# First pair of an attention kernel: the order of its maxima, score blocks, P·V groups and loads

## The chip, the cores and the metric

The kernel runs on one core of a Trainium2 chip. The metric is device time in microseconds (us) from start to end of one launch. PE is TensorE (matmul), DVE is VectorE, ACT is ScalarE, POOL is GpSimd, and SP is the engine whose queue issues most DMAs here. Each engine works through its own instructions in the order in which they stand.

## The reference, cut to what matters

Attention with queries averaged in pairs, then two mixture-of-experts layers, of which this change touches nothing:

```python
q_pool = q.reshape(B, H, S // 2, 2, D).mean(axis=3)       # B 4, H 8, S 1152, D 64
scores = scale * np.matmul(q_pool, k.transpose(0, 1, 3, 2))
scores = scores - np.max(scores, axis=-1, keepdims=True)
attn = np.exp(scores)
attn = attn / (np.sum(attn, axis=-1, keepdims=True) + 1e-09)
x = np.matmul(attn, v)                                    # then moe(x), then soft moe
```

## The kernel before

The 32 heads go in 16 pairs (`p` 0 to 15, the two heads `j` of a pair side by side). All operands of a pair are split into a high part and a remainder: `KS` holds the keys' high part in its upper 64 rows and their remainder in the lower 64, `QS` the queries' high part twice, `QL` the queries' remainder, `KH` the keys' high part again. Three sets of these exist, and pair `p` uses set `p % 3`.

**Maxima.** A query's maximum has to be known before its exponentials. `maxpiece` makes one product of 128 queries with 384 keys on PE (line 198) and reduces it on DVE (line 200). A pair has 27 pieces: per head nine for queries 0 to 383 (blocks 0 to 2, pieces 0 to 17 of the two heads), three for block 3, and three for block 4, which the two heads share (through the tile `QB`). `maxred` gathers the results in `MXZ` (lines 207 and 209), a small matmul turns it round (`nps`, line 229 for the first pair, 216 for the others), and DVE writes the maxima as extra rows of `QL` (lines 236 and 241, or 218 and 221). Only then can the second matmul of a score block run.

**Score blocks.** A pair has 36 score blocks, one for each half of the queries (`u`), each of nine key blocks (`c`) and each head (`j`). Block number is called position below. A block is a matmul `S1` (line 247), a matmul `S2` (line 253, which needs `QL` with the maxima) and an exponential on ACT (line 257) into `e`. Three PSUM buffers hold blocks, three others hold pieces.

**P·V groups.** After every six blocks PE makes a group of twelve products with V (line 267), and POOL adds up the sums of `e` (lines 278 and 280, 1.4 us each).

**The order.** Everything stands as the loops write it: a table gives, for each position, what is issued behind that block. While the blocks of pair `p` run, the pieces of pair `p + 1` are worked off between them (in the first pair from position `P1[0]` on), the operands of pair `p + 2` are prepared (`prep`, whose functions are: two casts of K into `KC`, the addition of the queries, the cast `QC`, two remainders `KL`, the remainder `QLc`), and the inputs of pair `p + 3` are loaded. `KC`, `KL`, `QC` and `QLc` go to their places in `KS`, `KH`, `QS` and `QL` by DMAs from SBUF to SBUF (line 149), which SP issues one after the other.

**The start.** `first` loads and prepares pair 0 with no DMA copies, and prepares pair 1 (`prep1`). Before the loop the 18 pieces of blocks 0 to 2 of both heads are made and reduced, with a small filler matmul (`warm`) behind all but the first three. The four DMAs of lines 530, 531, 1479 and 1480 load small tables (`wgbd`, `modt`, `mb`); those of line 519 copy five rows of ones into the two other sets of `KH`.

Of the kernel before, what the change touches and what calls it, by code (L numbers as in the profile page):

```python
# [12 lines left out]
AX = mybir.AxisListType  # L13
# [25 lines left out]
QSTEP = 2  # L39
GS = 3  # L40
LAG = 3
EB = 9
CST = 3
P0 = (0, 6)
P1 = (11, 22)
SWARM = (0, 1, 1)
FE = (14, 16, 17)
PREP = (2, 8, 2, 8, 14, 20, 26)
PREP0 = (14, 16, 14, 18, 20, 24, 28)
MA1 = (0, 1, 2, 3, 4, 5, 6, 7, 9, 10, 11, 12, 13, 15, 16, 17, 18, 19, 21, 22, 23, 24, 25, 27)  # L50
MA = (0, 1, 3, 4, 5, 6, 7, 9, 10, 12, 13, 15, 16, 17, 18, 19, 21, 22, 23, 25, 27)
MB = (29, 30, 31, 33, 34, 35)
MR = (29, 32)
FA = (26, 28, 33)
FB = (14, 16, 17)
FC = 7
# [25 lines left out]
def attention(ctx, tc, g):  # L82
# [116 lines left out]
            slot = 4 * j + blk  # L199
        V.reduce_max(s["mxp"][:, slot, t:t + 1], mps[:, :384], axis=AX.X)  # L200

    def maxred(p, blks):
        s = st[p]
        Z = MXZ
        if min(blks) < 4:
            b0, b1 = min(blks), min(max(blks), 3) + 1
            V.reduce_max(Z[:, :, 64 + b0:64 + b1], s["mxp"][:, 0:8].rearrange("p (j b) t -> p j b t", j=2)[:, :, b0:b1], axis=AX.X)
        if 4 in blks:
            V.reduce_max(Z[:, :, 68:69], s["mxp"][:, 8:9].unsqueeze(1).to_broadcast([128, 2, 1, 3]), axis=AX.X)

# [9 lines left out]
        for j in range(2):  # L220
            V.tensor_mul(ql[64:69, j, 512:576], nv[:, j, 64 * j:64 * j + 64], mask[64:69, 4, 0:64])

    def maxrow0(p, spans):

        s = st[p]
        ql = s["QL"]
        nps = ps.tile([128, 512], F32, name="nps", tag="mx", bufs=3)
        for j in range(2):
            nc.tensor.matmul(nps[:69, j * 128:(j + 1) * 128], MXZ[:, j, :], ident, start=True, stop=True)
        for j in range(2):  # L230
            nv = nps[64:69, j * 128:(j + 1) * 128]
            for lo, hi in spans:
                blk, o = divmod(lo, 128)
                if (hi - lo) % 128 == 0:
                    a = (hi - lo) // 128
# [192 lines left out]
    def first():  # L428
# [66 lines left out]
        for m in range(3, 9):  # L495
            maxpiece(0, m)
            warm(SWARM[1])
        klo(P, 1, 0)
        qadd(P, 1, qq[0])
        qadd(P, 1, qq[1])  # L500
        klo(P, 1, 1)
        klo(P, 1, 2)
        for j in range(2):
            nc.scalar.copy(KH[0][0:64, j], kx[j][0:64])
        prep1 = prep(1, P)
        for j in range(2):
            ql(P, j, q2[0])
        load(2)
        for f in prep1[:4]:
            f()  # L510
        for j in range(2):
            qadd(P, j, q2[1])
            nc.scalar.copy(QB0[:, j, j * 64:(j + 1) * 64], qs0[:, j, 512:576])
            ql(P, j, q2[1])
        return prep1, warm

    prep1, warm = first()
    for i in (1, 2):
        nc.sync.dma_start(out=KH[i][64:69].bitcast(F32), in_=KH[0][64:69].bitcast(F32))
    prep1[6]()  # L520
    nc.gpsimd.memset(wgbd, 0.0)
    nc.gpsimd.memset(ones, 1.0)
    for m in range(9, NP0):
        maxpiece(0, m)
        warm(SWARM[2])
    maxred(0, [0, 1, 2])
    maxrow0(0, [(0, 256), (256, 288)])
    for f in prep1[4:6]:
        f()
    nc.sync.dma_start(out=wgbd[0:64, :, 0:E], in_=wg[0])  # L530
    nc.sync.dma_start(out=wgbd[64:128, :, E:2 * E], in_=wg[1])
    consts = g["route_consts"]()
# [1 line left out]
    for p in range(n + 1):  # L534
# [5 lines left out]
        mp = lambda q, m: (lambda: maxpiece(q, m))  # L540
        NP = len(pieces)
        if p == 0:
            for i, m in enumerate(range(NP0, NP)):
                at(P0[0] + i * P0[1] // 8, mp(0, m))
            at(P0[0] + P0[1] + 1, lambda: maxred(0, [3, 4]))
            at(P0[0] + P0[1] + 2, lambda: maxrow0(0, [(288, 384), (384, 512), (512, 576)]))
            for i, m in enumerate([24, 25, 26] + list(range(24))):
                at(P1[0] + i * P1[1] // NP, mp(1, m))
            for i in range(3):
                at(33 + i, mp(2, 24 + i))  # L550
        elif p + 1 < n:
            for pos, m in zip(MA1, range(24)) if p == 1 else zip(MA, range(3, 24)):
                at(pos, mp(p + 1, m))
            if p + 2 < n:
                for pos, m in zip(MB, (24, 25, 26, 0, 1, 2)):
                    at(pos, mp(p + 2, m))
# [2 lines left out]
                at(pos, f)  # L559
        if p < n:  # L560
            if p + 1 < n:
                late = 3 if p == 0 else 0
                at(MR[0] + late, lambda: maxred(p + 1, [0, 1, 2, 3, 4]))
                at(MR[1] + late, lambda: maxrow(p + 1))
            late = 4 if p in (0, n - 1) else 0
            at(FA[0] + late, lambda: fin0(p, 0))
            at(FA[1] + late, lambda: fin1(p, 0))
# [70 lines left out]
            break  # L638

        units = [(u, c, j) for u in range(2) for c in range(NKB) for j in range(2)]  # L640
        for z in units[:3]:
            S1(p, *z)
        for pos, z in enumerate(units):
# [12 lines left out]
                        queue.pop(0)[1]()  # L656
            if pos == LAG - 1 and p > 0:
                group(p - 1, 2 * NKB // GS - 1)
            elif pos >= 2 * GS and pos % (2 * GS) == LAG - 1:
                group(p, pos // (2 * GS) - 1)  # L660
            if pos == 3 and p + 3 < n:
                if p == 0:
                    load_v(2)
                load(p + 3)
# [962 lines left out]
```

## Time and profile before

| | |
|---|---|
| time, median of 3 runs | 829.63 us (827.89 to 830.55) |
| the profiled execution, own time | 833.58 us |
| its span | 831.9 us |
| PE busy over the span | 798.0 us (96%) |
| DVE busy | 571.0 us (69%) |
| ACT busy | 466.9 us (56%) |
| POOL busy | 542.3 us (65%) |

A row of a timeline gives the start in us, the duration in us, the engine, the line, the operation, out<-in with the tiles' names, and how many instructions were merged; in brackets stands the idle time of the engine ahead of it and what ended it. PE's rows overlap, since matmuls are pipelined: the distance between two starts tells more than the durations. A row of the windows gives a stretch and the busy time of each engine in it, and after them the granted clock of PE as a share of 2.4 GHz.

### The profile page before, as it was taken

Reading aid. Unit: us, or ns where it says so; the run is one execution under the profiler, and the core shown is the slowest. Engines: PE = TensorE matmul, PEld = TensorE weight load, DVE = VectorE, ACT = ScalarE, POOL = GpSimd, SP = SyncE. Lnnn points to the kernel's source line nnn. Section 1 sums busy time; section 2 is a strip of 40 time slices with the busy share of each in tenths; the row PEclk is TensorE's granted clock in tenths of the full one; section 3 lists DMA queues with packets and bytes.
Section 4 is the critical chain, followed back from the end, with each engine's and each line's share of the span. In section 5 each row is a group of like instructions: output and inputs, shape, how many; then the busy total and the mean of one; then the engine's idle time right before and its main releaser. Section 6 shows DMA issues by size and latency. Waiting matters only on the chain. (4 is left out here: it accounts for less than half of the span.)

```text
span 831.9 us, 16156 instructions
## 1 busy us (share of the span) xinstructions
PE 798.0 (96%) x5808; PEld 612.5 (74%) x5808; DVE 571.0 (69%) x1177; ACT 466.9 (56%) x1107; POOL 542.3 (65%) x501
## 2 busy tenths in 40 slices
PE   5799999999999999999999999999999999999997
PEld 4567777777677676777666668798898988887456
DVE  7587777668777976877878786665665666665252
ACT  5456565657756558666547872554654545553123
POOL 6778899999888977879879962445446454450100
PEclk9899999999999999999999999999999999999998
DMA  9776558684664585566453212677776877757897
GB/s 317 218 198 160 159 150 218 156 224 137 144 161 145 133 213 157 159 145 172 117 130 102 87 42 79 241 253 274 255 266 218 303 238 271 269 189 243 280 391 228
DMA packets 57898, 163.13 MB, mean 196 GB/s; under 512 B 14474, under 2 KB 21962, under 8 KB 53706
## 3 DMA queue, kind: packets, MB, share of 16 engines
q1 hardware_dynamic: 41460, 97.01, 41.3%
q0 software_dynamic: 13760, 47.60, 17.1%
q10 hardware_dynamic: 2592, 17.43, 5.8%
q8 instruction: 47, 0.77, 0.4%
q14 instruction: 39, 0.32, 0.1%
HBM read 110.71 MB, written 10.90 MB: 146 GB/s over the span
## 5 line engine op out<-in xcount | busy, mean ns | idle before, releaser
L280 POOL TENSOR_TENSOR acc<-acc,e 128x576 f32<-128x576 f32 x214 | 315.9, 1476 | 28.2 <-ACT e L257 13.7
L257 ACT ACTIVATE e<-sc 128x288 f32<-128x288 f32 x576 | 224.3, 411 | 142.3 <-PE sc L253 120.3
L200 DVE TENSOR_REDUCE mxp<-mps 128x1 f32<-128x384 f32 x432 | 220.2, 549 | 99.5 <-PE mps L198 94.3
L247 PE MATMUL sc<-QS,KS 128*128 128x288 f32 x576 | 185.0, 329 | 3.0 <-ACT e L257 2.8
L253 PE MATMUL sc<-QL,KH 69*128 69x288 f32 x576 | 169.8, 297 | 1.5 <-DVE QL L218 1.2
L267 PE MATMUL pv<-e,V 128*64 128x288 f32 x1152 | 162.4, 417 | 0.0
L247 PEld LDWEIGHTS sc<-QS,KS 128*128 128x128 f32 x576 | 109.0, 190 | 52.3 <-issue 26.7
L198 PE MATMUL mps<-KS,QS 128*128 128x384 f32 x384 | 134.7, 355 | 13.1 <-ACT QS L463 7.3
L727 POOL DMA_INDIRECT wraw<-in_w,widx x72 | 73.0, 1013 | 109.9 <-DVE wlo L749 92.5
L267 PEld LDWEIGHTS pv<-e,V 128*64 128x64 f32 x1152 | 74.6, 137 | 63.8 <-issue 25.9
L749 DVE TENSOR_TENSOR wlo<-wraw,whi 128x512 fp32r<-128x512 f32 x144 | 95.9, 689 | 22.6 <-ACT whi L748 19.8
L253 PEld LDWEIGHTS sc<-QL,KH 69*128 69x128 f32 x576 | 109.1, 190 | 1.9 <-DVE QL L218 1.4
L748 ACT CAST whi<-wraw 128x512 fp32r<-128x512 f32 x144 | 84.1, 619 | 14.8 <-DMA wraw<-in_w,widx 10.4
L198 PEld LDWEIGHTS mps<-KS,QS 128*128 128x128 f32 x384 | 73.9, 193 | 17.1 <-ACT QS L463 7.7
L757 PE MATMUL hp<-xh,whi 128*128 128x256 f32 x288 | 81.9, 284 | 0.4 <-ACT xh L743 0.4
L758 PE MATMUL hp<-xl,whi 128*128 128x256 f32 x288 | 80.9, 281 | 1.4 <-DVE xl L744 1.4
L759 PE MATMUL hp<-xh,wlo 128*128 128x256 f32 x288 | 80.6, 280 | 0.0
L764 ACT ACTIVATE hh<-hp 128x256 fp32r<-128x256 f32 x72 | 27.7, 385 | 80.5 <-PE hp L759 54.5
L278 POOL TENSOR_TENSOR acc<-e 128x576 f32<-128x576 f32 x31 | 45.0, 1450 | 35.9 <-ACT e L257 35.8
L765 DVE SCALAR_TENSOR_TENSOR hl<-hp,hh 128x256 fp32r<-128x256 f32 x72 | 30.5, 423 | 48.5 <-ACT hh L764 41.2
L771 PE MATMUL yp<-whi,hh 128*128 128x512 f32 x144 | 59.6, 414 | 0.2 <-ACT hh L764 0.2
L758 PEld LDWEIGHTS hp<-xl,whi 128*128 128x128 f32 x288 | 54.1, 188 | 4.8 <-DVE xl L744 2.2
(366 smaller groups left out, 1237.5 us busy)
## 6 DMA issues: line engine op xcount, KB each, us to landing
mw<-in_m2w ACTq DMA_DIRECT2D x16, 1024.0 KB
mw<-in_m2w SPq DMA_DIRECT2D x16, 1024.0 KB
V<-in_vT SPq DMA_DIRECT2D x16, 576.0 KB
KX<-in_kT SPq DMA_DIRECT2D x15, 576.0 KB
QX<-in_qT SPq DMA_DIRECT2D x15, 576.0 KB
KS<-KC SPq DMA_DIRECT2D x30, 288.0 KB
KH<-KC SPq DMA_DIRECT2D x30, 288.0 KB
QS<-QC SPq DMA_DIRECT2D x60, 144.0 KB
```

Source lines behind the costliest of these rows:

```text
L198: nc.tensor.matmul(mps[:, :384], s["QS"][:, j, blk * 128:(blk + 1) * 128], s["KS"][:, j, ks], start=True, stop=True)
L200: V.reduce_max(s["mxp"][:, slot, t:t + 1], mps[:, :384], axis=AX.X)
L247: nc.tensor.matmul(sc[:, :NU], s["KS"][:, j, c * 128:(c + 1) * 128], s["QS"][:, j, u * NU:(u + 1) * NU], start=True, stop=False)
L253: nc.tensor.matmul(sc[:, :NU], s["KH"][0:69, j, c * 128:(c + 1) * 128], s["QL"][0:69, j, u * NU:(u + 1) * NU], start=False, stop=True)
L257: nc.scalar.activation(s["e", u, c][:, j], sc[:, :NU], AF.Exp, scale=SM)
L267: nc.tensor.matmul(pv[j * 64:(j + 1) * 64, :NU], s["v"][:, j, c, :], e[:, j], start=(c == 0), stop=(c == NKB - 1))
L280: eng.tensor_add(s["acc", u], s["acc", u], s["e", u, c])
L748: nc.scalar.copy(hi, x)
L749: nc.vector.tensor_sub(lo, x, hi.bitcast(F32))
L757: nc.tensor.matmul(hp, wh[:, c], xh[:, k], start=(k == 0), stop=False)
L758: nc.tensor.matmul(hp, wh[:, c], xl[:, k], start=False, stop=False)
L759: nc.tensor.matmul(hp, wl[:, c], xh[:, k], start=False, stop=(k == DM // 128 - 1))
```

## The change

It touches the first pair alone, and the operands of the second pair that are prepared beside it.

- Ahead of the loop one piece less than half is made: pieces 0 to 9 instead of 0 to 17 (`NJ1 = 1`), and the maxima of head 0 alone are gathered and turned (`js`). The eight other pieces of head 1 stand behind positions 0 to 7, and its gathering behind position 7.
- The blocks of the first half come in another order: nine of head 0, then nine of head 1, where they alternated.
- Pieces 18 to 26 stand behind positions 9 to 15 (they stood behind 0 to 5), the second pair's 27 pieces behind positions 17 to 32 (they stood behind 11 to 32). The groups stand behind positions 14, 17, 20, 26 and 32 (8, 14, 20, 26 and 32).
- In `first` POOL makes `QL` of head 0 before the queries' additions of head 1. Of `prep1`, the remainders `KL` of the second pair move ahead of `QC`; `QC` stands behind position 4, `QLc` behind 5. So their copies stand behind the small tables in SP's queue.
- The preparation of the third pair starts later (`PREP0`); gathering and turning the second pair's maxima stand behind positions 32 and 33 (32 and 35); the loads of the fourth pair stand behind position 8 (3).

```diff
+PV0 = (14, 17, 20, 26, 32)
-P0 = (0, 6)
-P1 = (11, 22)
+P0 = (9, 6)
+P1 = (17, 16)
+NJ1 = 1
-PREP0 = (14, 16, 14, 18, 20, 24, 28)
+PREP0 = (19, 20, 16, 22, 24, 26, 30)
+MR0 = (32, 33)
...
         klo(P, 1, 0)
+        ql(P, 0, q2[0])
         qadd(P, 1, qq[0])
...
-        for j in range(2):
-            ql(P, j, q2[0])
-        load(2)
-        for f in prep1[:4]:
-            f()
-        for j in range(2):
-            qadd(P, j, q2[1])
+        ql(P, 1, q2[0])
+        load(2)
+        c = q2[1]
+        for j in range(2):
+            P.tensor_add(qs0[:, j, c], qx[:, j, 0, c], qx[:, j, 1, c])
+        for i in (0, 1, 2, 4, 5):
+            prep1[i]()
+
+        def rest(j):
+            nc.scalar.copy(QS[0][:, j, c], qs0[:, j, c])
             nc.scalar.copy(QB0[:, j, j * 64:(j + 1) * 64], qs0[:, j, 512:576])
-            ql(P, j, q2[1])
-        return prep1, warm
+
+        return [(1, lambda: rest(0)), (2, lambda: rest(1)), (3, lambda: ql(P, 0, c)), (3, lambda: ql(P, 1, c)), (4, prep1[3]), (5, prep1[6])], warm
...
-    for m in range(9, NP0):
+
+    maxred(0, [0, 1, 2], slice(0, 1))
+    for m in range(9, 9 + NJ1):
         maxpiece(0, m)
         warm(SWARM[2])
-    maxred(0, [0, 1, 2])
-    maxrow0(0, [(0, 256), (256, 288)])
+    maxrow0(0, [(0, 256), (256, 288)], (0,))
...
+            for pos, f in early:
+                at(pos, f)
+            for i, m in enumerate(range(9 + NJ1, NP0)):
+                at(i, mp(0, m))
+            at(7, lambda: maxred(0, [0, 1, 2], slice(1, 2)), lambda: maxrow0(0, [(0, 256), (256, 288)], (1,)))
...
+        if p == 0:
+            units[:18] = [(0, c, j) for j in range(2) for c in range(NKB)]
...
-            if pos == 3 and p + 3 < n:
+            if pos == (3 if p else 8) and p + 3 < n:
```

PE at the end of the start, before (`mps` is a piece, `nps` the turned maxima, `sc` a block by `S1` or, from `QL`, by `S2`; names end in buffer numbers, and `KS_138`, `KH_141`, `QS_144`, `QL_147` are the first pair's):

```order
L198 MATMUL mps<-KS_138,QS_144 128x384
L479 MATMUL warm<-ident 128x128
L229 MATMUL nps<-ident,MXZ 69x128 x2
L247 MATMUL sc<-QS_144,KS_138 128x288 x3
L253 MATMUL sc<-QL_147,KH_141 128x288
L198 MATMUL mps<-KS_138,QS_144 128x384 x2
L253 MATMUL sc<-QL_147,KH_141 128x288
```

PE at the same place after the change:

```order
L201 MATMUL mps<-KS_138,QS_144 128x384
L482 MATMUL warm<-ident 128x128
L232 MATMUL nps<-ident,MXZ 69x128
L250 MATMUL sc<-QS_144,KS_138 128x288 x3
L256 MATMUL sc<-QL_147,KH_141 128x288
L201 MATMUL mps<-KS_138,QS_144 128x384
L256 MATMUL sc<-QL_147,KH_141 128x288
```

The rows are alike but for one turned head instead of two; before, 18 pieces stand ahead of them, now 10, and the next pieces are head 1's.

SP's queue from the second pair's first copy to the first of the later loads, before (`KS_139`, `KH_142`, `QS_145` and `QL_148` are the second pair's):

```order
L149 DMA KH_142<-KC 64x1152
L149 DMA QS_145<-QC 64x576 x4
L149 DMA QB<-QC 64x64 x2
L519 DMA KH_142<-KH_141 5x2304
L519 DMA KH_143<-KH_141 5x2304
L149 DMA QL_148<-QLc 64x576 x2
L149 DMA KS_139<-KL 64x1152 x2
L530 DMA wgbd<-in_wg 64x4x8
L531 DMA wgbd<-in_wg 64x4x8
L1479 DMA modt<-in_mod 96x48
L1480 DMA mb<-in_mbias 96x16
L133 DMA V_162<-in_vT 128x1152
```

The same stretch of SP's queue after the change:

```order
L152 DMA KH_142<-KC 64x1152
L152 DMA KS_139<-KL 64x1152 x2
L526 DMA KH_142<-KH_141 5x2304
L526 DMA KH_143<-KH_141 5x2304
L535 DMA wgbd<-in_wg 64x4x8
L536 DMA wgbd<-in_wg 64x4x8
L1493 DMA modt<-in_mod 96x48
L1494 DMA mb<-in_mbias 96x16
L152 DMA QS_145<-QC 64x576 x4
L152 DMA QB<-QC 64x64 x2
L152 DMA QL_148<-QLc 64x576 x2
```

The `KL` copies went ahead, and the copies of `QC` into `QS` and `QB`, which were first, now stand behind the small tables.

PE where the second pair's pieces begin, before (`mps<-KC,QB` are the second pair's three shared pieces, which come first):

```order
L229 MATMUL nps<-ident,MXZ 69x128 x2
L267 MATMUL pv<-e,V_160 64x288 x6
L247 MATMUL sc<-QS_144,KS_138 128x288
L253 MATMUL sc<-QL_147,KH_141 128x288
L247 MATMUL sc<-QS_144,KS_138 128x288
L253 MATMUL sc<-QL_147,KH_141 128x288
L247 MATMUL sc<-QS_144,KS_138 128x288
L253 MATMUL sc<-QL_147,KH_141 128x288
L195 MATMUL mps<-KC,QB 128x384 x2
L247 MATMUL sc<-QS_144,KS_138 128x288
```

PE where they begin after the change:

```order
L232 MATMUL nps<-ident,MXZ 69x128 x2
L250 MATMUL sc<-QS_144,KS_138 128x288
L256 MATMUL sc<-QL_147,KH_141 128x288
L198 MATMUL mps<-KC,QB 128x384 x2
L270 MATMUL pv<-e,V_160 64x288 x6
L250 MATMUL sc<-QS_144,KS_138 128x288
L256 MATMUL sc<-QL_147,KH_141 128x288
```

Before, they stand behind position 11 and one group; now behind position 17, with one group ahead of them and the second right behind the first two.

## Rows read from the trace of the kernel before

**Rows 1.** Windows: stretch, busy us (instructions) of each engine, PE's clock, DMA, GB/s.

```profile
30.00:40.00 10.00, 6.78 (x28) 4.61 (x29) 2.30 (x6) 2.00 (x5) 5.24 (x5) 0.66 0.86 286
60.00:70.00 10.00, 10.00 (x72) 7.13 (x69) 7.35 (x13) 6.75 (x16) 8.36 (x10) 1.00 0.61 152
33.00:38.80 5.80, 5.58 (x20) 3.41 (x21) 1.12 (x2) 1.19 (x3) 1.52 (x2) 0.50 0.90 323
```

**Rows 2.** Timeline of PE over the first pair.

```profile
19.77 0.37 PE L253 MATMUL sc<-QL,KH 69*128 69x288 f32 x1 [0.31 <-ACT QB L513]
...
29.15 0.29 PE L253 MATMUL sc<-QL,KH 69*128 69x288 f32 x1
33.22 0.66 PE L198 MATMUL mps<-KS,QS 128*128 128x384 f32 x1 [3.78 <-DMA KS<-KL]
...
34.61 3.15 PE L267 MATMUL pv<-e,V 128*64 128x288 f32 x12
...
41.74 1.68 PE L267 MATMUL pv<-e,V 128*64 128x288 f32 x12
...
55.51 0.38 PE L216 MATMUL nps<-ident,MXZ 128*69 128x128 f32 x2
...
57.62 0.40 PE L253 MATMUL sc<-QL,KH 69*128 69x288 f32 x1 [1.21 <-DVE QL L218]
```

**Rows 3.** Timeline of DVE over the same stretch.

```profile
11.02 7.06 DVE L200 TENSOR_REDUCE mxp<-mps 128x1 f32<-128x384 f32 x15
18.18 0.17 DVE L207 TENSOR_REDUCE MXZ<-mxp 128x6 f32<-128x18 f32 x1
...
42.73 0.76 DVE L173 TENSOR_TENSOR KL<-KX,KC 128x576 fp32r<-128x576 f32 x1
...
46.42 1.52 DVE L173 TENSOR_TENSOR KL<-KX,KC 128x576 fp32r<-128x576 f32 x1
...
52.97 0.18 DVE L207 TENSOR_REDUCE MXZ<-mxp 128x8 f32<-128x24 f32 x1
```

**Rows 4.** Timeline of POOL.

```profile
13.70 1.98 POOL L466 TENSOR_TENSOR QL<-qs,QS 64x384 fp32r<-64x384 f32 x2
...
18.09 0.58 POOL L466 TENSOR_TENSOR QL<-qs,QS 64x192 fp32r<-64x192 f32 x1 [0.48 <-ACT QS L463]
...
19.69 0.59 POOL L466 TENSOR_TENSOR QL<-qs,QS 64x192 fp32r<-64x192 f32 x1 [0.46 <-ACT QS L463]
20.25 1.41 POOL L179 TENSOR_TENSOR QLc<-qs,QC 128x576 fp32r<-128x576 f32 x1
...
21.77 2.81 POOL L173 TENSOR_TENSOR KL<-KX,KC 128x576 fp32r<-128x576 f32 x2
...
44.40 1.43 POOL L278 TENSOR_TENSOR acc<-e 128x576 f32<-128x576 f32 x1 [2.18 <-ACT e L257]
```

**Rows 5.** Timeline of ACT.

```profile
14.03 1.24 ACT L153 CAST KC<-KX 128x576 fp32r<-128x576 f32 x2
```

**Rows 6.** Timeline of SP's queue: the DMAs as they are issued.

```profile
15.29 0.55 SPq L149 DMA_DIRECT2D KS<-KC  x1
...
19.18 3.85 SPq L149 DMA_DIRECT2D QS<-QC  x4
23.13 1.18 SPq L149 DMA_DIRECT2D QB<-QC  x2
24.41 1.58 SPq L519 DMA_DIRECT2D KH<-KH  x2
...
28.16 1.18 SPq L149 DMA_DIRECT2D KS<-KL  x2
29.38 0.85 SPq L530 DMA_DIRECT2D wgbd<-in_wg  x1
...
32.61 0.37 SPq L133 DMA_DIRECT2D V<-in_vT  x1
```

**Rows 7.** DMA packets of the stretch from 20 to 26 us.

```profile
DMA packets 602, 1.25 MB, mean 208 GB/s; under 512 B 213, under 2 KB 213, under 8 KB 601
```

**Rows 8.** Waits of SP's queue in the first 62 us: total us, times, longest.

```profile
SPq L133 <- DMA qx<-in_q: 1.2, 1, 1.2
```

More of the change, by code (lines that the diff above doesn't have):

```diff
@@ L200, in maxpiece, with maxred @@
         V.reduce_max(s["mxp"][:, slot, t:t + 1], mps[:, :384], axis=AX.X)
-    def maxred(p, blks):
+    def maxred(p, blks, js=slice(0, 2)):
         s = st[p]
@@ L206, in maxred @@
             b0, b1 = min(blks), min(max(blks), 3) + 1
-            V.reduce_max(Z[:, :, 64 + b0:64 + b1], s["mxp"][:, 0:8].rearrange("p (j b) t -> p j b t", j=2)[:, :, b0:b1], axis=AX.X)
+            V.reduce_max(Z[:, js, 64 + b0:64 + b1], s["mxp"][:, 0:8].rearrange("p (j b) t -> p j b t", j=2)[:, js, b0:b1], axis=AX.X)
         if 4 in blks:
@@ L221, in maxrow, with maxrow0 @@
             V.tensor_mul(ql[64:69, j, 512:576], nv[:, j, 64 * j:64 * j + 64], mask[64:69, 4, 0:64])
-    def maxrow0(p, spans):
+    def maxrow0(p, spans, js=(0, 1)):
         s = st[p]
@@ L227, in maxrow0 @@
         nps = ps.tile([128, 512], F32, name="nps", tag="mx", bufs=3)
-        for j in range(2):
+        for j in js:
             nc.tensor.matmul(nps[:69, j * 128:(j + 1) * 128], MXZ[:, j, :], ident, start=True, stop=True)
-        for j in range(2):
+        for j in js:
             nv = nps[64:69, j * 128:(j + 1) * 128]
@@ L505, in first @@
         prep1 = prep(1, P)
+        ql(P, 1, q2[0])
+        load(2)
+        c = q2[1]
         for j in range(2):
-            ql(P, j, q2[0])
-        load(2)
-        for f in prep1[:4]:
-            f()
-        for j in range(2):
-            qadd(P, j, q2[1])
+            P.tensor_add(qs0[:, j, c], qx[:, j, 0, c], qx[:, j, 1, c])
[3 more added lines that the diff above has]
+            nc.scalar.copy(QS[0][:, j, c], qs0[:, j, c])
             nc.scalar.copy(QB0[:, j, j * 64:(j + 1) * 64], qs0[:, j, 512:576])
-            ql(P, j, q2[1])
-        return prep1, warm
-    prep1, warm = first()
+        return [(1, lambda: rest(0)), (2, lambda: rest(1)), (3, lambda: ql(P, 0, c)), (3, lambda: ql(P, 1, c)), (4, prep1[3]), (5, prep1[6])], warm
+    early, warm = first()
     for i in (1, 2):
         nc.sync.dma_start(out=KH[i][64:69].bitcast(F32), in_=KH[0][64:69].bitcast(F32))
-    prep1[6]()
     nc.gpsimd.memset(wgbd, 0.0)
     nc.gpsimd.memset(ones, 1.0)
-    for m in range(9, NP0):
+    maxred(0, [0, 1, 2], slice(0, 1))
+    for m in range(9, 9 + NJ1):
         maxpiece(0, m)
         warm(SWARM[2])
-    maxred(0, [0, 1, 2])
-    maxrow0(0, [(0, 256), (256, 288)])
-    for f in prep1[4:6]:
-        f()
+    maxrow0(0, [(0, 256), (256, 288)], (0,))
     nc.sync.dma_start(out=wgbd[0:64, :, 0:E], in_=wg[0])
@@ L545, in attention @@
             at(P0[0] + P0[1] + 1, lambda: maxred(0, [3, 4]))
-            at(P0[0] + P0[1] + 2, lambda: maxrow0(0, [(288, 384), (384, 512), (512, 576)]))
+            at(P0[0] + P0[1] + 1, lambda: maxrow0(0, [(288, 384), (384, 512), (512, 576)]))
             for i, m in enumerate([24, 25, 26] + list(range(24))):
@@ L561, in attention @@
             if p + 1 < n:
-                late = 3 if p == 0 else 0
-                at(MR[0] + late, lambda: maxred(p + 1, [0, 1, 2, 3, 4]))
-                at(MR[1] + late, lambda: maxrow(p + 1))
+                mr = MR if p else MR0
+                at(mr[0], lambda: maxred(p + 1, [0, 1, 2, 3, 4]))
+                at(mr[1], lambda: maxrow(p + 1))
             late = 4 if p in (0, n - 1) else 0
@@ L658, in attention @@
                 group(p - 1, 2 * NKB // GS - 1)
-            elif pos >= 2 * GS and pos % (2 * GS) == LAG - 1:
+            elif p == 0 and pos in PV0:
+                group(p, PV0.index(pos))
+            elif p and pos >= 2 * GS and pos % (2 * GS) == LAG - 1:
                 group(p, pos // (2 * GS) - 1)
-            if pos == 3 and p + 3 < n:
+            if pos == (3 if p else 8) and p + 3 < n:
                 if p == 0:
```

## Prediction

> **What bounds the kernel now.** I read the windows first. From 60 us on PE is busy in all of each stretch at full clock; from 30 to 40 us it is busy for 6.78 of 10 us, and its clock is 0.66 [rows 1]. So there is time to win at the start, and what is won there stays won, because every later pair is PE's own work. I measure the start by one event: the first `S2` of the second pair, at 57.62, against 19.77 for the first pair [rows 2]. The 37.9 us between them are to be compared with about 27 to 28 us for a steady pair (an estimate from the full PE rows behind it).
>
> The timeline of PE shows where the difference lies [rows 2]. At 29.15 it ends position 12; then it idles 3.78 us, until the DMA `KS<-KL` has landed, because the second pair's first piece needs it. Behind the stall its clock is at 0.50, the 1.2 GHz level, until 38.8 [rows 1], and a group takes 3.15 us where 1.68 is usual [rows 2]. At the end 1.21 us go to the maxima of the second pair. The timeline of DVE shows the second limit [rows 3]: a reduction costs 7.06 / 15 = 0.47 us, so the 18 pieces ahead of the loop take 8.5 us in which PE mostly waits, and the second pair's 27 take 12.7 us, which cannot start before their operands have landed.
>
> **The start of the first pair: 4.2 us earlier.** Nine reductions fewer stand ahead of the first `MXZ`: 9 x 0.47 = 4.2, so it comes at 18.18 - 4.2 = 14.0 [rows 3]. `S2` followed 1.6 us behind [rows 2, 3], so PE starts on blocks at about 15.5 instead of 19.8. The eight fillers that go cost nothing: PE waits for DVE there. On ACT, POOL's early `QL` (half of 1.98 [rows 4]) delays the casts of head 1's queries by 1.0 us, and with them `KC` from 15.27 to 16.3 [rows 5]. The first exponentials wait for that and PE, with three buffers, for them, some 1 us; DVE then has head 1's eight reductions to do, and between its `MXZ` and position 9 the 1.6 us latency shows again, less one block. Both delays are hidden by what follows.
>
> **When PE reaches the second pair's pieces: about 28.5.** Before, 13 positions with 12 pieces and one group took 29.15 + 0.3 - 19.77 = 9.7 us [rows 2]. Now 18 positions, 17 pieces and one group come first, so some 13 us: 15.5 + 13 = 28.5. That is about as early as before, with five positions more done and, counted with those ahead of the loop, three pieces fewer.
>
> **When their operands land: 34.0 instead of 33.2.** This decides, and it is SP's queue. POOL ends `KL` at 24.58 before [rows 4]; two `QL` (0.58 + 0.59, and waits of 0.48 + 0.46), `QLc` (1.41) and two memsets (0.1) now stand behind it, so `KL` is ready at 24.58 - 3.6 = 20.9. SP has issued `KC`'s four copies by then (3.9 us from 16.3 [rows 6]) and waits. From 20.9 it issues `KL` (28.16 to 29.38, 1.2), the rows of ones (1.6), the four small tables (29.38 to 32.61, 3.2), and only at 27.0 can it come to `QS` (3.85) and `QB` (1.18 and gaps): done at 32.2 [rows 6]. So what moved ahead is what was late before, and what moved back becomes as late. From issue to landing I have only the bound of `KL`: issued by 29.34, PE runs at 33.22, 3.9 us [rows 2, 6]. `QB` is 16 KB a copy and `KL` 288, so I take half, 1.9: landed at 34.1, in round numbers 34.0. Bounds: below, `QS` at the pace of `KL` (four in 2.4 us) and nothing for the landing, 30.7; above, 32.2 + 3.9 = 36.1. One more wait lies within these: SP holds a DMA back until an earlier one on the same semaphore has landed (1.2 us in [rows 8]); there are eight such semaphores, and `QS` now follows `KL` and the tables on them. At 208 GB/s [rows 7] a 288 KB copy (0.295 MB) takes 1.4 us, six take 8.5, and from 16.3 they end at 24.8 at the earliest, up to 3.9 later with the landing: up to 28.7, against the 28.0 at which the second `QS` copy would be issued.
>
> So the stall is not removed: it moves from position 12 to position 17 and grows from 3.8 to some 5.5 us. The clock falls again, I take it, until about 38.8 as before.
>
> **From there to the second pair: DVE.** Two pieces go at once, then the second group stands in the way at the low clock (3.15), then a block and a piece: 34.0 + 0.7 + 3.15 + 0.7 = 38.5. There are 25 reductions left, 25 x 0.47 = 11.8. The two `KL` of the third pair stand among them, 0.76 + 1.52 = 2.3 [rows 3]. Behind the third group DVE starves about 1.0 (1.68 less what the three buffers hold). The sum is 53.6, against 52.97 before for the same `MXZ` [rows 3]. PE is not the limit there: 1.6 pieces a position cost DVE 0.75 us, and PE, at 72 matmuls in 10 us [rows 1], some 0.5 for 3.6 matmuls. From `MXZ` to the turning took 55.51 - 52.97 = 2.5 us before; two positions with pieces, about 0.9, now fall out of it: 53.6 + 1.6 = 55.2. From turning to `S2` it is 57.62 - 55.51 = 2.1 [rows 2]: 57.3. Of the two `KL` the short one ran while POOL was idle (up to 44.40 [rows 4]), the long one beside POOL's work. If both now run beside POOL, another 0.8 us comes on top, 58.1; I take the middle, 57.8.
>
> The Trainium skill (SBUF — State Buffer, section "Who interferes with whom") says that a DVE operation with two SBUF inputs and a POOL operation shut each other out for a whole instruction. The two durations above agree with it; by that rule alone both `KL` would be long, and the sum would be 58.1.
>
> **Sum.** 57.8 - 57.62 = +0.2 us. Everything behind is moved by that. The third pair's copies are not late by it: the fourth pair's loads go out at about 34.5 instead of 32.61 [rows 6], and the third pair's first piece, at position 33, is wanted at about 55. The sum is made against the profiled execution (833.58, span 831.9), which would become 833.8; the median of the runs shown is 829.63, and I carry the difference to it: **829.8 us**.
>
> **Rivals.** *The stall shrinks and the clock holds.* If `QS` is issued at the quick pace and lands at once, at 31 to 32, PE idles 2.5 to 3.5 us; if the clock then stays at 2.4 GHz, the second group costs 1.68: 31.5 + 0.5 + 1.7 + 0.4 = 34.1, and then the same 11.8 + 2.3 + 1.0 + 1.6 + 2.1 = 18.8, so 52.9, 4.7 us earlier; at 32.5 with the low clock it is 56.3, 1.3 earlier. I price the rival near its better end, 4.2 earlier: 825.4. For it speaks that the first blocks do come 4.2 us earlier; against it that even the lower bound of 30.7 lies behind PE's arrival at 28.5, and that an idle time of 3.78 was enough for the fall [rows 1, 2].
>
> The Trainium skill (TensorE: Matmul & The Clock Gate, section "What's actually happening") says that the clock gate does not restart with the kernel, so that the moment of a change differs from run to run. No single trace shows that; by it the fall could be missed in some runs, which is the case just priced.
>
> *The landing is late and the clock stays low.* If the small tables and the rows of ones hold back the semaphores that `QS` and `QB` need, the second pair lands at the upper bound, 36.1: a stall of 7.6 us. From 36.1, 0.7 + 3.15 + 0.7 gives 40.7, and if the low clock covers the third group too, DVE starves 2.4 instead of 1.0: 40.7 + 11.8 + 2.3 + 2.4 + 1.6 + 2.1 = 60.9, with long `KL` 61.7. That is 3.3 to 4.1 us later: 833.3. It decides from a landing at about 36. For it speaks that small packets are many in that stretch (213 of 602 under 512 B [rows 7], before the tables even come), against it that `QB` was not waited for before.
>
> *The change does not do what it says*: the score blocks could be held behind ACT's casts, so that head 0 does not run ahead. That would cost or save nothing here, since PE would still arrive before 34.0; it is part of the forecast.
>
> **How the numbers follow.** Forecast (stall moved, 828 to 831.5): 0.57. Shorter stall (824.5 to 828): 0.25. Late landing (831.5 to 834.5): 0.18. A measurement of this kernel can tell about 0.3%, 2.5 us, from no change. Most of the first rival's chance lies beyond that and a little of the forecast's own spread, so faster 0.25; slower 0.17; within 0.58. The range reaches to the price of the faster rival and nearly to that of the slower: 825.4 to 833.0.
>
> **What would show it.** In the changed trace: first `S2` at about 15.5; PE idle from 28 to 29 until about 34, ended by a DMA (`QB<-QC`) rather than `KS<-KL`; a clock of 0.50 behind it; SP's `QS` copies from 27 on; the `MXZ` of the second pair at 53 to 54.5; its first `S2` at 57 to 58.5. I am wrong if the stall is under 2.5 us, if the clock stays full, or if PE rather than DVE paces positions 18 to 32.

## The result and the profile after

The changed kernel takes 833.9 us (median of 5 runs, 832.78 to 836.07), the kernel before beside it 828.46: ratio 1.0055, 95% interval 1.0041 to 1.0068, so about 4.6 us slower (the medians lie 5.4 us apart). The forecast was 829.8, its range ended at 833.0. The profiled execution of after took 836.07 us (span 834.3).

The stretches of after (columns as in [rows 1]): from 30 to 40 us the clock is again low on the mean, and PE idles.

```profile
core 0: us, PE busy (x) PEld busy (x) DVE busy (x) ACT busy (x) POOL busy (x), PEclk, DMA share, GB/s
30.00:40.00 10.00, 6.70 (x29) 3.99 (x28) 3.19 (x12) 1.38 (x4) 7.38 (x6) 0.66 0.86 259
60.00:70.00 10.00, 10.00 (x65) 7.34 (x66) 7.59 (x17) 7.12 (x17) 7.15 (x9) 1.00 0.32 92
```

The timeline of PE in after (start, duration, what; in brackets the idle time ahead and what ended it), the answer to [rows 2]:

```profile
16.86 0.37 PE L256 MATMUL sc<-QL,KH 69*128 69x288 f32 x1 [0.32 <-DVE QL L244]
...
21.50 0.44 PE L232 MATMUL nps<-ident,MXZ 128*69 128x128 f32 x2 [0.91 <-DVE MXZ L210]
...
30.95 0.66 PE L232 MATMUL nps<-ident,MXZ 128*69 128x128 f32 x4 [0.65 <-DVE MXZ L212]
...
34.53 0.98 PE L198 MATMUL mps<-KC,QB 128*128 128x384 f32 x2 [2.65 <-DMA QB<-QC]
35.44 3.15 PE L270 MATMUL pv<-e,V 128*64 128x288 f32 x12
...
41.18 1.68 PE L270 MATMUL pv<-e,V 128*64 128x288 f32 x12
...
59.93 0.40 PE L256 MATMUL sc<-QL,KH 69*128 69x288 f32 x1
```

The first score block of the first pair comes 2.9 us earlier than before (19.77), that of the second pair 2.3 later (57.62). Between them PE waits 2.65 us for `QB`, and a group at 35.44 costs 3.15 us at half clock (0.50, the 1.2 GHz level, from 33.0 to 39.9). SP's queue in after, to be read against [rows 6]: `QS` and `QB` stand behind `KL`, the rows of ones and the tables.

```profile
20.66 1.51 SPq L152 DMA_DIRECT2D KS<-KL  x2
22.27 1.63 SPq L526 DMA_DIRECT2D KH<-KH  x2
24.00 1.33 SPq L535 DMA_DIRECT2D wgbd<-in_wg  x1
25.38 1.48 SPq L536 DMA_DIRECT2D wgbd<-in_wg  x1
...
28.07 3.36 SPq L152 DMA_DIRECT2D QS<-QC  x4
31.48 1.24 SPq L152 DMA_DIRECT2D QB<-QC  x2
```

DVE in after, against [rows 3]: a subtraction at 9.99 that takes 1.70 us (the same one takes 0.73 in the kernel before), and the second pair's maxima from 39.73 to the `MXZ` at 56.27 (52.97 before).

```profile
9.99 1.70 DVE L476 TENSOR_TENSOR KS<-V,KS 64x384 fp32r<-64x384 f32 x1
...
39.73 2.42 DVE L203 TENSOR_REDUCE mxp<-mps 128x1 f32<-128x384 f32 x5 [3.48 <-PE mps L198]
43.54 3.34 DVE L203 TENSOR_REDUCE mxp<-mps 128x1 f32<-128x384 f32 x7 [1.39 <-PE mps L201]
46.91 1.95 DVE L176 TENSOR_TENSOR KL<-KX,KC 128x576 fp32r<-128x576 f32 x1
...
50.18 0.74 DVE L176 TENSOR_TENSOR KL<-KX,KC 128x576 fp32r<-128x576 f32 x1
...
54.75 1.49 DVE L203 TENSOR_REDUCE mxp<-mps 128x1 f32<-128x384 f32 x3 [0.58 <-PE mps L201]
56.27 0.18 DVE L210 TENSOR_REDUCE MXZ<-mxp 128x8 f32<-128x24 f32 x1
```

A second loss lies where nothing was changed, in the last expert block near the end of the program. Its timeline on PE in after, and then in a second profile of the kernel before:

```profile
780.12 1.06 PE L1375 MATMUL hp<-mw,siT 128*32 128x512 f32 x7 [0.89 <-DVEq L1562]
782.62 7.48 PE L1375 MATMUL hp<-mw,siT 128*32 128x512 f32 x65 [1.44 <-issue]
790.03 1.09 PE L1325 MATMUL tp<-ident,hs 128*128 128x128 f32 x8
791.05 6.21 PE L1375 MATMUL hp<-mw,siT 128*32 128x512 f32 x56
```

```profile
774.73 7.93 PE L1361 MATMUL hp<-mw,siT 128*32 128x512 f32 x72 [0.78 <-DVEq L1548]
782.59 1.09 PE L1311 MATMUL tp<-ident,hs 128*128 128x128 f32 x8
783.62 6.21 PE L1361 MATMUL hp<-mw,siT 128*32 128x512 f32 x56
```

The same 128 matmuls take 17.15 us from the first start to the last end instead of 15.10; in after PE stands still behind the seventh of them, and no engine and no transfer is named, only "issue".

Fifteen of the eighteen profiles stand in the table; the other three are in their sections below. The first exponential of a pair on ACT marks its start; "wait" is PE's idle time ahead of the second pair's first pieces, "low" the stretch at clock 0.50 that begins within 3 us of it, "experts" the time from the end of the last exponential of the 16 pairs to the start of the block, and "block" the 128 matmuls above.

| kernel (section below) | wait, us | low, us | 2nd pair | 7th pair | experts | block | span |
|---|---|---|---|---|---|---|---|
| before, first profile | 3.78 `KL` | 6.83 | 58.1 | 202.9 | 280.4 | 15.10 | 831.9 |
| before, second | 2.63 | none | 54.8 | 201.6 | 276.9 | 15.10 | 826.9 |
| before, third | 3.3 | 3.41 | 56.5 | 203.4 | 275.9 | 15.10 | 827.9 |
| before, fourth | 3.0 | 3.41 | 56.7 | 203.6 | 275.9 | 15.10 | 828.1 |
| after, first | 2.65 `QB` | 6.83 | 60.4 | 207.8 | 276.0 | 17.15 | 834.3 |
| after, second | 3.29 | 6.83 | 59.6 | 206.9 | 276.4 | 17.04 | 833.8 |
| tables late | none | none | 54.9 | 202.3 | 276.7 | 19.00 | 831.2 |
| three fillers | none | none | 57.3 | 204.7 | 278.3 | 15.10 | 832.2 |
| fillers in the wait | filled | none | 58.4 | 205.8 | 275.9 | 15.10 | 830.9 |
| tables late, three fillers | none | none | 55.6 | 203.0 | 276.0 | 15.10 | 828.3 |
| early `QL` undone | 4.58 | 6.83 | 59.7 | 207.1 | 276.6 | 18.71 | 835.9 |
| before, 9 fillers fewer | 1.7 | none | 55.4 | 202.3 | 276.0 | 16.67 | 828.5 |
| before, `KL` early | none | none | 57.5 | 206.1 | 276.0 | 15.10 | 830.7 |
| the same, loads late | none | none | 51.3 | 200.6 | 277.1 | 15.10 | 826.2 |
| the same, `KL` of two pairs later | none | none | 51.4 | 197.4 | 276.0 | 15.10 | 821.9 |

### The profile page after: what moved, and what is told of

Same layout as the page of the kernel before. It is cut to its first block, busy times and chain, and to the rows that moved or that the text cites. A ratio compares the mean times of both kernels' runs of the same rounds, so it can differ in the third digit from the quotient of the medians.

```text
span 834.3 us, 16124 instructions
## 1 busy us (share of the span) xinstructions
PE 800.0 (96%) x5792; PEld 612.7 (73%) x5792; DVE 576.6 (69%) x1178; ACT 468.0 (56%) x1107; POOL 545.0 (65%) x501
## 5 line engine op out<-in xcount | busy, mean ns | idle before, releaser
L201 PE MATMUL mps<-KS,QS 128*128 128x384 f32 x384 | 136.7, 360 | 11.4 <-ACT QS L466 7.0
L779 DVE SCALAR_TENSOR_TENSOR hl<-hp,hh 128x256 fp32r<-128x256 f32 x72 | 30.5, 424 | 44.7 <-ACT hh L778 44.7
L785 PE MATMUL yp<-whi,hh 128*128 128x512 f32 x144 | 59.6, 414 | 0.0
L787 PE MATMUL yp<-whi,hl 128*128 128x512 f32 x144 | 56.9, 395 | 0.0
```

Source lines behind the costliest of these rows:

```text
L201: nc.tensor.matmul(mps[:, :384], s["QS"][:, j, blk * 128:(blk + 1) * 128], s["KS"][:, j, ks], start=True, stop=True)
```

## The experiments

**SP's queue.** The changed kernel with the rows of ones and the tables behind the queries' copies:

```diff
-    (the two KH<-KH copies, wgbd, modt, mb issued ahead of the loop)
+            at(6, tables)
```

> The changed kernel, with the two ones-row copies of KH and the transfers of the expert tables (wgbd, modt, mb) issued on SP's queue behind the copies of QS, QB and QL instead of ahead of them. Theory A (SP's queue order sets when QB lands, and QB's landing sets the start of the second pair's maxima): QB lands at about 29.4 us instead of 34.4, the 2.65 us wait of PE that ended with it at 34.53 is gone, the clock does not fall there, the second pair's first score block starts at about 55 us instead of 59.9, and the time falls by 4 to 5 us against the changed kernel, to 826 to 829 us. Rival B (VectorE's own order sets the maxima of the second pair, the transfer only stands beside it): the wait goes, the maxima end where they did, the first score block stays at 59 to 60 us, time 833 to 834 us. A result between the two shows how much of the delay is each.

PE's timeline of this run shows the pieces without a wait, and a group at full clock behind them:

```profile
29.95 0.66 PE L232 MATMUL nps<-ident,MXZ 128*69 128x128 f32 x4 [0.65 <-DVE MXZ L212]
...
30.72 0.52 PE L198 MATMUL mps<-KC,QB 128*128 128x384 f32 x2
31.16 1.68 PE L270 MATMUL pv<-e,V 128*64 128x288 f32 x12
```

`QB` landed at 29.4 and 30.5, the second pair began 5.5 us earlier than in after: theory A. The time fell by less than forecast, to 832.34 us (ratio to before 1.0021, 1.0009 to 1.0033), and its profile shows why: the last block took 19.00 us, 1.85 more than in after, with a stop of 1.17 us and behind it 3.41 us at clock 0.50 (777.7 to 781.1), and the experts 0.7 more.

**Fillers in the start.** `SWARM = (0, 1, 1)` became `(0, 3, 3)` in the changed kernel.

> The changed kernel with three filler matmuls instead of one behind each piece of the first pair's maxima, nothing else. Rival C (TensorE's late rise to the full clock in the start, 15.98 us in the changed kernel against 11.53, is what delays the second pair): the clock rises some 2 to 4 us earlier, and the second pair's first score block starts about 2 us earlier, time 831 to 832 us. Theory A (the landing of QB sets it): the early blocks move, the wait for QB grows by as much, the first score block of the second pair stays at 59.9 us within 0.5, time 833 to 834 us.

833.92 us (1.0041, 1.0024 to 1.0058), second pair 3.1 us earlier. Neither side had it right. The clock rose 1.5 us earlier, but PE reached the second pair's pieces 1.8 us later, at 33.7 instead of 31.9, when `QB` was as good as there: no wait, no fall, and the group behind costs 1.68. Being later saved 3 us, and the block is back at 15.10. The time shows little of these 5 us: its profile gives back 2.3 in the experts and 0.7 behind the block, where nothing was edited, and why is not shown.

**Fillers in the wait.** In after, 14 filler matmuls ahead of the second pair's first piece.

```diff
+            at(P1[0], delay)
```

> The changed kernel with 14 filler matmuls on TensorE ahead of the first piece of the second pair's maxima, so in its wait for QB; they also bring the number of TensorE's instructions ahead of the experts to that of the kernel before (21 fillers there, 7 in the changed kernel). Theory G (the wait's idle time lets the clock fall, and that costs 3 us; the length of PE's program costs 2 us in the last expert block): the clock holds at 33 to 40 us in the profile, the second pair starts at 57 to 57.5, and the block hp<-mw,siT takes 15.10 us instead of 17.15; time 831 to 832 us. Rival H (the block's extra time comes from the transfers' phase and not from PE's program): it stays over 16.5 us.

The count in it is wrong: the kernel before has 15 fillers, one behind each of the pieces 3 to 17, and the changed kernel 7; this run has 21.

831.93 us (1.0026, 1.0014 to 1.0038). The fillers took 3.29 us, the pieces came at 34.83 instead of 34.53, and still the second pair began 2.0 us earlier, since the group cost 1.68 and not 3.15. The block is back at 15.10 here too.

**Both together**, tables late and three fillers:

> The changed kernel with the expert tables and KH rows late and with three fillers instead of one behind each piece (two edits that were run apart, 832.3 and 833.9 us). Theory G: the second pair starts at 54 to 55 us as with the tables late alone, and the block hp<-mw,siT takes 15.10 us instead of the 19.0 there; so the time falls to 829 to 830 us. Rival H: the block stays over 16.5 us and the time at 832.

829.46 us; ratio 1.0000 (0.9991 to 1.0009). With the wait, the fall and the block's loss gone, the changed kernel equals before, which keeps its own wait for `KL`; the 1.3 to 1.9 us by which its first pair starts earlier than before's buy nothing.

**The start.** In after, `ql(P, 0, q2[0])` was put back behind the queries' additions.

> The changed kernel with head 0's first query residue back behind the queries' additions on POOL and ACT, as in the kernel before; nothing else. Theory (the early residue shut VectorE's KS subtraction out for 1 us and delayed the casts; but QB's landing at 34.4, set by SP's order, decides): that subtraction takes 0.73 us again instead of 1.70, the first score block comes 0.5 to 1.5 us earlier than 16.86, QB lands within 0.5 us of 34.4, the wait for it grows by as much, and the time stays within 1 us of 833.9. Rival (the start decides): the second pair starts 1 us or more earlier.

The subtraction takes 0.73 us again, the first score block comes at 15.34, `QB` lands at 33.34 and 33.68, the wait grows to 4.58, the second pair's exponential is at 59.7: 835.13 us (1.0065, 1.0046 to 1.0084). As the theory said, but that `QB` landed 0.7 to 0.9 us earlier, where 0.5 was allowed, and that the time is 1.2 us over 833.9, where 1 was allowed; its block took 18.71 us, again with 3.41 us at clock 0.50 behind the stop. The clock of the start rose at 11.69 here and at 15.98 in after, so the 1.5 us of the first score block are not the subtraction's alone.

**The block.** The kernel before with `SWARM = (0, 1, 0)`, so 6 fillers instead of 15 (after has 7; the expectation miscounts them as 6 of 21):

> The kernel before without the 15 fillers behind the later pieces of the first pair's maxima (6 of 21 stay; the changed kernel has 7). Theory G (with so few of TensorE's instructions ahead of it, the last expert block waits for instructions): the 128 matmuls hp<-mw,siT take 16.7 to 19 us instead of 15.10, and the time rises by some 2 us for that alone. Rival H (the block's extra time belongs to something else in the changed kernel): 15.10 us. In the start the fillers' going may delay the clock's rise; that is read from the second pair's start and kept apart.

831.81 us (1.0029, 1.0016 to 1.0042), and the stop appears in the kernel before:

```profile
774.64 1.07 PE L1361 MATMUL hp<-mw,siT 128*32 128x512 f32 x8 [0.83 <-DVEq L1548]
777.07 7.07 PE L1361 MATMUL hp<-mw,siT 128*32 128x512 f32 x64 [1.36 <-issue]
```

With 15 fillers or more, in twelve profiles, the block takes 15.10; with 6 or 7, in six profiles (one not in the table, 16.73), 16.67 to 19.00. Taking fillers out of before brings the stop, adding them to after removes it: so the number of PE's instructions ahead decides, as theory G said. That the stop is a wait for instructions, as it also said, is not shown.

**The kernel before once more.** Three further profiles of it (the fourth with the same expectation as the third), and one of after:

> The kernel before, unchanged, profiled once more. In the first profile of it the third POOL addition ahead of sel<- at 162.2 us took 2.49 us and VectorE's KL subtraction beside it 0.74, while in the changed kernel and in the four runs so far POOL's took 1.41 and VectorE's 1.53 to 1.58, and PE waited 1.0 us after that. Theory D1 (the kernel before keeps its gain of some 2 us in the fourth to sixth pairs in every execution): the first exponentials of all pairs stand within 0.3 us of the first profile's. Rival D2 (who gets through first is settled anew in each execution, and the first profile of before was a lucky one): the pairs from the fifth on start some 2 us later than in the first profile, and the extra 2.6 us of the changed kernel are not its own.

> The kernel before, profiled a third time. Either the clock holds behind the wait for KL (second pair at 54.8 us, as in the second profile) or it falls for 3.4 or 6.8 us (56.5 to 58.1, as in the first). Theory: holding or the short fall is the usual course, since the median of its times, 829.5 to 830.9, lies 3 to 4 us under the first profile's 833.58 and near the second's 828.59.

> The changed kernel, unchanged, profiled once more. A second profile of the kernel before (826.9 us of span) had no fall of the clock behind its wait for KL and started the second pair at 54.8 us instead of 58.1, so the first profile of before was a slow execution. Theory F (the changed kernel has the same two courses, and each lies 2 to 2.5 us behind the like course of before): if the clock holds behind the wait for QB, the second pair starts at 57 us, and if it falls, at 60.4. In both, the 128 matmuls hp<-mw,siT of the last expert block take over 16.5 us (17.15 in the first profile; 15.10 in all profiles of before). Rival: the second pair starts as in before, 54.8, where the clock holds, and the block takes 15.1.

The second profile of before, the wait of [rows 2] and what followed:

```profile
32.46 0.42 PE L198 MATMUL mps<-KS,QS 128*128 128x384 f32 x1 [2.63 <-DMA KS<-KL]
...
33.25 1.68 PE L267 MATMUL pv<-e,V 128*64 128x288 f32 x12
...
54.31 0.40 PE L253 MATMUL sc<-QL,KH 69*128 69x288 f32 x1 [1.21 <-DVE QL L218]
```

```profile
30.00:40.00 10.00, 7.52 (x48) 5.29 (x48) 5.85 (x12) 4.44 (x11) 7.06 (x5) 1.00 0.84 275
```

These executions took 828.59, 829.94 and 829.92 us, the first 833.58: the prediction was built on the longest of the four, the one with the longest fall. But the fall is not what made it the longest. By the end of the last exponential the first profile is 0.5 us ahead of the third; then it loses 4.4 us in the layers of experts, between 584 and 742 us, where nothing was changed. First profile of before, then its third, the last exponentials on ACT and the block on PE:

```profile
498.50 0.71 ACT L257 ACTIVATE e<-sc 128x288 f32<-128x288 f32 x2 [0.24 <-PE sc L253]
...
779.57 7.93 PE L1361 MATMUL hp<-mw,siT 128*32 128x512 f32 x72 [0.73 <-DVEq L1548]
```

```profile
499.00 0.71 ACT L257 ACTIVATE e<-sc 128x288 f32<-128x288 f32 x2 [0.23 <-PE sc L253]
...
775.61 7.93 PE L1361 MATMUL hp<-mw,siT 128*32 128x512 f32 x72 [0.72 <-DVEq L1548]
```

In this stretch PE waits 2.0 us in the first profile, mostly for a DVE subtraction (four times 0.34 us), and not at all in the third; what slowed it was not traced. The expectation of the third profile read the long fall from the execution's time; the time does not show it. The second profile of after (835.57 us) had the long fall again; a course of after without it was not caught.

These profiles settle another point. Between the first profiles of the two kernels the lag of after grows from 2.3 us at the second pair to 4.9 at the seventh. In the fifth pair DVE's second `KL` took 0.74 us in that profile of before; in every later profile with that order, of before as well, 1.53 to 1.58. First profile of before, then its second:

```profile
160.20 0.74 DVE L173 TENSOR_TENSOR KL<-KX,KC 128x576 fp32r<-128x576 f32 x1
...
161.49 0.82 DVE L382 TENSOR_TENSOR lg<-lg,sm 96x48 f32<-96x48 f32 x1
...
162.70 0.19 DVE L383 SCALAR_TENSOR_TENSOR rtmp<-lg,wt 96x48 f32<-96x48 f32 x1
```

```profile
156.92 1.56 DVE L173 TENSOR_TENSOR KL<-KX,KC 128x576 fp32r<-128x576 f32 x1
...
158.87 1.21 DVE L382 TENSOR_TENSOR lg<-lg,sm 96x48 f32<-96x48 f32 x1
...
160.47 0.97 DVE L383 SCALAR_TENSOR_TENSOR rtmp<-lg,wt 96x48 f32<-96x48 f32 x1
```

In the first, POOL's addition beside it took 2.49 us and not 1.42: there POOL waited, everywhere else DVE does, and PE 1.0 us for it. Against the first one, the three later profiles of before lose 2.0 us over these pairs, and after loses 2.6; 0.6 of after's is in the first three blocks of its second pair. Its next group starts 1.69 us behind the first `S2` (59.93 to 61.62), in the third profile of before 1.13. In after DVE makes five reductions in a row from 60.18 (2.41 us), two of them for the third pair's pieces; in before these two stand ahead of the second pair's `QL` rows, and the change turns the maxima two positions earlier. That PE waits for these two is argued from the order, not shown. Theory D1 fell, and D2 held for the time between the pairs, though not for all their starts: the second profile, without a fall, is ahead of the first from the second pair on.

**A pure delay.** The kernel before with 24 fillers at position 35 of the first pair:

> The kernel before with 24 filler matmuls (128 columns) on TensorE at position 35 of the first pair, as a pure delay of some 2.5 to 3 us; they compute nothing that is used. Theory D (a shift of the pairs against POOL and the transfers changes waits in the fourth to sixth pairs, as the changed kernel's lag grew from 2.3 us in the second pair to 4.9 us in the seventh): the delay x at the second pair is another at the seventh, by some 1 to 2.5 us more or less. Rival E (a shift is carried unchanged, and the extra 2.6 us of the changed kernel have another cause): the lag of the first exponentials is x in every pair, and the time is 828.5 + x, some 831 us.

836.07 us (1.0061, 1.0041 to 1.0080); second pair at 61.2, seventh at 208.0. The delay is longer than the 2.5 to 3 us expected. Against the third profile of before, which has the same 3.41 us of low clock, that is 4.7 and 4.6 us: carried unchanged, so rival E. Against the first profile of before it would have looked like theory D.

**The loads alone, and `KL` moved.** The kernel before with the fourth pair's loads at position 8, and after with `PREP`'s `KL` at 23 instead of 20:

> The kernel before with the last part of the change alone: the fourth pair's loads and the third pair's V at position 8 of the first pair instead of 3. Theory (this part costs nothing by itself: SP reaches them behind the tables either way): the copies of the third pair and the second pair's first score block stand within 0.5 us of before, time within 1 us of 830. Rival (it brings the loads into the copies of the third pair or delays them): the second pair starts over 1 us later or earlier.

> The changed kernel with the second half of KL at position 23 instead of 20 in the second and later pairs, nothing else. Theory D (in the fourth pair VectorE's two-input subtraction meets POOL's additions and loses 0.8 us, and two small operations behind it 0.4 and 0.8): the meeting is at another place, the growth of the lag in the fifth and sixth pairs (1.1 and 0.9 us) changes by at least 0.5 us in one of them. Rival (the growth there is from the transfers or the expert work, whatever VectorE's order): the lag grows by 2.0 us over these pairs within 0.2.

The first: 830.77 us, ratio 0.9999 (0.9986 to 1.0012), second pair at 56.5 as in two profiles of before; that part of the change does nothing by itself. The second: the lag to the first profile of before goes from 2.8 us at the fifth pair to 2.5 at the seventh instead of growing by 2, and 1.5 to 1.6 us are lost in each of two later pairs; its single timing is 836.46 us.

**A faster kernel.** In the kernel before, `KL` is made on POOL ahead of the last two `QL`, and the tables go behind `QL`:

```diff
+        for f in prep1[4:6]:
+            f()
         for j in range(2):
             ql(P, j, q2[1])
```

> The kernel before, with KL's two residues made on POOL ahead of the last two query residues, and the KH ones rows and expert tables issued behind QL; nothing of the tested change. Theory A: KL lands at about 29 us instead of 33.0, the 3.78 us wait of PE for it that ended at 33.2 shrinks to nothing, the clock does not fall behind it, and the first score block of the second pair starts at 53 to 55 us instead of 57.6: 3 to 5 us faster than the kernel before, some 825 us. Rival B (VectorE's reductions set it): gain under 1 us, the start stays at 57 to 58 us. If the gain is there at the second pair and not at the end, it was given back in the later pairs.

832.33 us (1.0016, 1.0003 to 1.0030). The wait for `KL` went and the maxima were done at 46.8, as theory A had it, but then:

```profile
52.67 0.66 PE L195 MATMUL mps<-KC,QB 128*128 128x384 f32 x1 [4.25 <-DMA QB<-QC]
```

Around this wait the clock was at 0.50, from 51.0 to 61.2. The third pair's copies, now earlier, were issued right behind the fourth pair's loads; the queues were full (DMA share 1.03 from 35 to 40) and `KS<-KC` took 11.6 us to land. So the loads went behind the copies:

```diff
-            if pos == 3 and p + 3 < n:
+            if pos == (3 if p else 29) and p + 3 < n:
```

> The kernel of the run with KL early and the tables late, with the fourth pair's loads (and the third pair's V) issued at position 29 of the first pair instead of 3, so behind the third pair's copies. In the run without this VectorE's maxima of the second pair were done at 46.9 us (53.0 before), and then PE waited 4.25 us for the third pair's QB, whose copies stood on the queues behind 2.4 MB of loads and landed at 52.6. Theory: QB of the third pair lands before 46, the wait is gone, the clock does not fall at 51, and the second pair's first score block starts at 50.5 to 52 us instead of 57.5: some 5 us faster than that run, 826 to 828 us. Rival (the copies are late by their sources, not by the queue): the wait for QB stays within 1 us of 4.25 and the time at 832 us. Another rival: the loads now come late for the fourth pair's KC, and the second pair waits for KX at its position 2.

826.40 us, ratio 0.9952 (0.9937 to 0.9968); second pair at 51.3. Of the 6.8 us that the second pair is ahead of the first profile of before, 2.6 are given back within it; PE waits 2.0 us for DVE there. Last, `KL` at position 23 in the fifth and sixth pairs alone:

> The fastest kernel so far (before, with KL early and tables and loads late, 826.4 us), with the second half of KL at position 23 instead of 20 while the fifth and sixth pairs run. With that position in all pairs the changed kernel lost nothing in these two (lag +2.8 us before, +2.5 behind them) but lost 1.5 to 1.6 us in each of two later ones and 0.7 in a third. Theory D (who meets whom on VectorE and POOL): the 1.5 and 0.45 us that these pairs lose go, and no other pair changes: the seventh pair starts 1.9 us earlier than in that run, time 824.5 us. Rival: the loss moves to the next pairs, and the time stays within 0.5 of 826.4.

824.92 us, ratio 0.9948 (0.9934 to 0.9961), the fastest kernel here, though not told apart from the one without this edit by these intervals. From the fifth pair's start to the seventh's it takes 58.6 us instead of 60.7, with no wait of PE left there.

## Why the prediction was wrong

**The base was one execution (wrong, some 1.6 us).** "57.8 - 57.62 = +0.2 us ... I carry the difference to it": the difference was made against a profile with 6.83 us of low clock behind its wait, and carried to a median. The other three profiles have 3.41 or none, and over all four the second pair of before starts at 56.5 on the mean, not 58.1. The text had a hint that the profile was not the usual one, 833.58 against a median of 829.63, and treated the 4 us as a constant; these 4 us lie in the experts, though, and by the end of its pairs that profile had made good its late second pair, 2.0 us of it in the fifth and sixth. It also quoted the Trainium skill (TensorE: Matmul & The Clock Gate, section "What's actually happening") that the moment of a change differs from run to run; the four profiles agree (rise at 11.5, 13.7, 12.4 and 13.4 us), and it used that for the changed kernel only, not for the base.

**The last block (missing, 2.0 us).** "The eight fillers that go cost nothing" looked only at the place where they stood. The block hundreds of us behind costs 2.0 us more without them; taking nine away from before costs it 1.6.

**The landing (right).** `QB` ended the wait at 34.53, 34.0 was forecast, by the very queue order that was worked out: `KL` 20.66 (20.9 forecast), `QB` issued by 32.7 (32.2). The fall behind it and the group of 3.15 came as forecast.

**PE's arrival (mis-sized by 3.4 us, without effect).** 28.5 was forecast, 31.9 measured. The first score block came at 16.86 and not 15.5: the early `QL` on POOL held DVE's subtraction for 1 us, and the clock rose only at 15.98; with the early `QL` undone both are gone and it is 15.34. Not in the sum were the waits for `MXZ` (0.91, which the text named and called hidden, and 0.65) and 3.4 us of half clock from 22.8. All of it only shortens the wait for `QB`, to 2.65 us where some 5.5 was forecast.

**From the landing to the second pair (mis-sized by 2.1 us).** To the first of the last 25 reductions 38.5 was forecast, 39.73 measured: 0.5 from the wait's end, 0.7 because the block and the pieces too ran at half clock. From there to `MXZ` 15.1 was forecast, 16.5 measured: `KL` 2.69 for 2.3, DVE's idle time 1.97 for 1.0. From `MXZ` to the score block 3.66, as forecast. The prediction took from the Trainium skill's rule (SBUF — State Buffer, section "Who interferes with whom", that a DVE operation with two inputs in SBUF and a POOL operation shut each other out) that both `KL` would be long. One was (1.95, behind a POOL operation that started 0.07 us ahead of it); the other took 0.74, starting 0.02 us ahead of POOL's, which took 1.99 instead of 1.41: the trace agrees with the rule, but there it was POOL that waited.

**Everything behind is moved by that (right for the pairs but for 0.6 us in the second pair's first blocks).** The rest of the growth in the later pairs is before's own, seen in three of four profiles.

**The rivals.** The shorter stall with a full clock is what the kernel with late tables does; its second pair is 3.2 us ahead of the first profile of before, where the price was 4.2. The late landing named 833.3, near the result, but its cause did not occur.

The terms together, against the third and fourth profile of before, whose times are the median's: the second pair at 60.0 (mean of two) against 56.6, 3.4; 0.6 in the second pair; 2.0 in the block: 6.0 us, where the spans differ by 834.1 - 828.0 = 6.1. Against all four it is 5.4, since the first profile gained 2.0 in the pairs and lost 4.4 in the experts. The ratio says 4.6; both profiled executions of after (836.07 and 835.57) lie above its median, and what the shorter ones do differently no profile shows.

## What to carry to other kernels

Profile the base more than once before a difference of 0.3% is built on it, and take the execution whose time is the median's; a clock fall behind one wait is a matter of that execution. Compare the profiles stretch by stretch: the execution with the longest fall was long for another reason. When work is moved ahead on a queue, write down what lands later for it: the gain here was in the queue's order (tables and loads behind what PE needs next), not in an earlier start. Instructions that cost nothing where they stand can matter far behind (here 8 of them, 2.0 us), so compare a far, unchanged stretch as well.

## What the runs showed of the hardware

- How many instructions stand ahead of a stretch of PE's program can decide whether it stops there: the last block takes 15.10 us with 15 or more fillers in the start and 16.67 to 19.00 with 6 or 7. The two longest of these (18.71 and 19.00) hold 3.41 us at clock 0.50 behind the stop, the other four none. That PE waits for its own instructions is a reading, not shown: in after a packet of 16 KB on the queue that the profile names "instruction" starts at 780.01 us, and PE, which began the block at 780.12, goes on at 782.62; in the second profile of before such a packet starts at 775.22, 0.5 us into the block, and nothing stops. The Trainium skill (Runtime: NRT & Kernel Launch, section "Instruction fetch mechanics") says that instructions are refilled in blocks of 16 KiB by a queue of their own, at a cost mostly hidden; the packet's size agrees, and if the stop is such a refill, the block lost 1.6 to 3.9 us by it here, low clock included. Which instruction waits for which packet the profile does not say.
- Waits of nearly the same length were followed by different clocks: 2.63 us in before by none of the low level, 2.65 in after by 6.83 us at 1.2 GHz, 3.0 and 3.3 in before by 3.41, 3.29 in after by 6.83. No row tells these apart.
- DVE's `KL` started 0.45 to 0.51 us behind a POOL addition in the fifth pair of every profile with that order: once POOL waited (2.49 instead of 1.42) and PE lost nothing, in the other executions DVE waited (1.53 to 1.58 instead of 0.74) and PE lost 1.0 us.
